# Attention two steps later in a fused attention and feed-forward kernel, its output projection behind the last down products, and the first weight scale formed in another order

## The chip, the cores and the metric

The kernel runs on one core of a Trainium2 chip. The metric is the device time of one execution in microseconds: 1605.36 us, the median of three runs (1605.04 to 1605.62). The engines' names are those of the profile: PE is the matrix engine TensorE, PEld its weight loads, DVE is VectorE, ACT is ScalarE, POOL is GpSimd, and SP is SyncE, whose queue issues every transfer (DMA) here. PSUM is the memory of eight banks into which PE writes and from which DVE and ACT fetch results ("evict" them). Moving a piece of work in one engine's program moves what stands behind it, since each engine works its program off in order.

## The reference

The input is x, 2048 rows of 576 numbers. Two blocks work on the same x, and a gate mixes them:

```python
g = sigmoid((x * gate_w).sum(-1, keepdims=True))
a = attention(x, wq, wk, wv, wo, beta)
b = (gelu(x @ w_gate) * (x @ w_up)) @ w_down      # 576 -> 4608 -> 576
return g * a + (1 - g) * b
```

The attention has 32 heads of 18 numbers. The 2048 rows form four segments of 512. Inside a segment a head has causal softmax attention. Beside that each head reads a memory M with a normalizer z, which sums phi(k) v over the segments before; the two are mixed by sigmoid(beta). The joined heads are multiplied by wo, the output projection.

## The kernel before

Numbers are held as pairs of 16-bit words, a high and a low part, and a product is three matmuls (high times high, high times low, low times high). A pair is made by an ACT copy (high) and a DVE or POOL subtraction (low); for weights this is `pair_of` (L108), after a scale that comes from the sum of the squares of the whole weight.

The work has three stages.

**Opening and projections** (about the first 220 us). PE first warms up and multiplies the unscaled x of segment 0 by the value weights (`first_words`, L509), into the banks dn, dn, V and pv for the first half of the columns (`va`) and G, U, st and st for the second half (`vb`), four blocks of 128 rows each. `put_rows` (L477) evicts such a bank: two ACT copies at once, and a DVE operation (L495, and L497 for the gate's column) that goes onto a list `later`; `finish_later` (L446) runs what is on the list. `stat_qk(j)` (L427) forms the sum of squares of one of nine weight tiles, on DVE or on ACT. `scale_sum` (L103) lets PE add those sums up over the partitions, into a bank that `spare` (L59) hands out by `turns`, and DVE reduces them and forms the scale. `make_qk(j)` (L439) makes the pair of tile j. `low_x` (L163) forms the low words of x, in three pieces. Then `project` (L450) multiplies tile j by x, into G, st, st and U in turn. The other three segments follow in the same way.

**The main loop** (from about 220 us) has 72 steps, `step(v)` (L1104). A step takes one tile f = v // 2 of 128 feed-forward columns and one half p of the rows. Four steps make a block fb of two tiles; i4 = v % 4 is the place in the block. The products with the gate and up weights use the banks V, G (named X) and U (named Y). `down` (L977) multiplies a block's hidden values (hh) by the down weights (paird), 32 calls of six matmuls each for a block, which are spread over the four steps of the next block as `early` and `late` (there are none in the first four steps). The last block's 32 follow behind the loop. The weights of the next tiles are scaled, summed and split on POOL and ACT in each step (`weights_first`, `weights_high`, `weights_low`), and `act_squares` takes squares on ACT, three of them at i4 = 1.

Between these stands attention, with k = v - LAG and LAG = 2 (L1260): in step v the scores of pair k (of its two segments) are formed (`scores`, L876, banks st and dn), DVE takes their maxima, ACT the exponentials (`powers`, L901) and the high parts, POOL the low parts (`pair_rows`, L911), SP issues two DMA transposes (`turn_rows`, L922; tiles ph to pt), and PE multiplies the result by the values (`values`, L928, bank pv) one step later for the first of the two segments and two steps later for the second. `normalize` scales the result. After four pairs the result of a group of heads is split and stored to DRAM (oa) by `result_high` (ACT, L961) and `result_low` (DVE and SP, L966). `load_head` (L842) loads the queries and keys of a pair two steps ahead, `load_v` (L859) the values of four pairs and what the memory gave (ob). Exponentials and gelu need different tables of ACT, which are loaded at each switch.

**The end.** At `LAST` = 2 * 32 + LAG + 1 attention's tiles are freed, and `turned` (L1235) fetches the stored results back, 16 blocks of 128 rows, turned by DMA (ot, ten of them at a time). `finish(0)` to `finish(4)` load the output weights (rows), take their squares, form their scale and make five pairs (wos), one call a step. Behind the loop, for each of 16 row blocks, two `down` and two output products (`chain_x`, 14 matmuls each, banks st) follow, and the block is stored.

In `tc.manual_schedule` the programs of PE, ACT, DVE and POOL have the order in which the code issues them; SP's order, and every order outside of it (the last loop, L1277 to L1288), is a scheduler's.

Of the kernel before, what the change touches and what calls it, by code (L numbers as in the profile page):

```python
# [10 lines left out]
F16 = mybir.dt.float16  # L11
# [32 lines left out]
def kernel(ctx: ExitStack, tc: tile.TileContext, xs, wqk, wv, wo, wgu, wd, beta, out):  # L44
# [58 lines left out]
    def scale_sum(i, st):  # L103
        t = wts.tile([P, 1], F32, name="sv", tag="sv", bufs=2)
        dve.tensor_reduce(t, sums(st), AX.X, OP.add)
        scale_of(i, t)

    def pair_of(t, r, sc):  # L108
        act.activation(t[:, 0, : r.shape[1]], r, AF.Copy, scale=sc)
        dve.scalar_tensor_tensor(t[:, 1, : r.shape[1]], r, sc, t[:, 0, : r.shape[1]], OP.mult, OP.subtract)  # L110

# [279 lines left out]
    with tc.tile_pool(name="prj", bufs=2, side="right", reuse_waits="tile") as pp:  # L391
# [35 lines left out]
        def stat_qk(j):  # L427
            square_sum(wst[:, 10 + j : 11 + j], raw_qk[:, j], j % 2)

# [8 lines left out]

        def make_qk(j):  # L439
            W[j] = pp.tile([P, 2, KT * P], F16, name="wp", bufs=9)  # L440
            pair_of(W[j], raw_qk[:, j], wsc[:, 0:1])

# [149 lines left out]
        with tc.manual_schedule(engines=ORDERED):  # L592
# [71 lines left out]
            for q in (2, 3):  # L664
                put_rows(0, q, 1, vb[q], usc, 1.0)
            x_raw.pop(0)
            dve.tensor_scalar(gh[:, 1], gh[:, 1], 1.0, None, OP.add)
            dve.reciprocal(gh[:, 0], gh[:, 1])
            dve.tensor_scalar(gh[:, 1], gh[:, 0], -1.0, 1.0, OP.mult, OP.add)
            finish_later()  # L670
            outscale(0, 1)

# [39 lines left out]
            def behind_rows(s, q):  # L712
                if s == 3:
                    if q < 3:
                        form_sums(1, q, -1)
                    if q == 0:
                        squares(0, 0, 0, act_square)
                    if q == 3:
                        rescale_words(2)
                        high_g(0, 0)  # L720
                        low_g(0, 0)

            def beside_products(s, j):
                if s == 0:
                    if j < 7:
                        make_qk(j + 2)
                    if j < 5:
                        make_v(j)
# [104 lines left out]
    with tc.tile_pool(name="keep", bufs=2, side="right", reuse_waits="tile") as kp, ExitStack() as tail:  # L833
# [270 lines left out]
        def step(v):  # L1104
# [137 lines left out]
        def finish(i):  # L1242
# [9 lines left out]
            if i == 2:  # L1252
                scale_sum(2, wst[:, 0:5])

                dve.tensor_scalar(gate[:, 2], gate[:, 0], wis[:, 2:3], wis[:, 3:4], OP.mult, OP.mult)
            if i >= 2:
                for k in ((0, 1), (2, 3), (4,))[i - 2]:
                    pair_of(wos[k], rows[k], wsc[:, 2:3])

        LAG = 2  # L1260
        LAST = 2 * H + LAG + 1
        with tc.manual_schedule(engines=ORDERED):
            for v in range(2 * NF):
                step(v)

                if v == LAST:
                    atn.close()
                    op_ = tail.enter_context(tc.tile_pool(name="outp", bufs=2, side="right", reuse_waits="tile"))
                if v >= LAST:
                    turned(2 * (v - LAST))  # L1270
                    turned(2 * (v - LAST) + 1)
                    finish(v - LAST)
            end_pair()
        turns.update(of=3)


        fb = NB - 1  # L1277
        for t in range(10, 16):
            turned(t)
        for t in range(16):  # L1280
            for n in range(2):
                down(fb, t, n)
            for n in range(2):
# [3 lines left out]
                dve.scalar_tensor_tensor(av, o[:, :NH], gate[:, 2, t : t + 1], av, OP.mult, OP.add)  # L1287
            sp.dma_start(out[t * P : (t + 1) * P, :], acc[:, t])  # L1288

# [39 lines left out]
```

## Time and profile before

| | us |
|---|---|
| median of three runs | 1605.36 |
| the profiled execution, its own time | 1605.14 |
| its span, first to last instruction | 1603.4 |
| PE busy in it | 1586.3 |
| ACT busy | 1166.0 |
| DVE busy | 1144.0 |
| POOL busy | 1128.2 |

A row of the timeline has the start in us from the span's start, the time in us, the engine, the line and the operation; x12 joins twelve instructions of a kind, and the brackets give the idle time of the engine just before, with what ended it. A row of the waits has the total in us, the number of times and the longest. A row of the stretches has the length, then for PE, PEld, DVE, ACT and POOL the busy time with the number of instructions, then the granted clock of TensorE, the DMA engines' busy share and GB/s. The end of a matmul is modelled: rows of back-to-back matmuls overlap, and the pace is read from one start to the next.

### The profile page before, as it was taken

The page shows a single profiled execution, that of the slowest core. Times are in us where ns is not written, and L with a number is a line of the kernel's source. Part 1 is how long each engine was busy: PE and PEld are TensorE (multiplying, and loading weights), DVE is VectorE, ACT ScalarE, POOL GpSimd, SP SyncE. Part 2 cuts the span into 40 slices and gives each one's busy share as a digit, 9 for nine tenths or more (in the row PEclk, how much of TensorE's full clock was granted, in tenths as well). Part 3 has the DMA queues.
Part 4 walks back from the last instruction along what each step waited for, and adds up shares of the span by engine and source line. Part 5 has one row for each costly group of instructions (what it writes and reads, how often), then busy time and mean ns, then how long its engine had stood idle before and what let it go on. Part 6 is the DMA issues. An engine that isn't in the chain of part 4 may idle for free.

```text
span 1603.4 us, 32611 instructions
## 1 busy us (share of the span) xinstructions
PE 1586.3 (99%) x11912; PEld 931.5 (58%) x11912; DVE 1144.0 (71%) x2957; ACT 1166.0 (73%) x1976; POOL 1128.2 (70%) x1091
## 2 busy tenths in 40 slices
PE   8999999899999999999999999999999999999999
PEld 5665754555555555555555555555555555555577
DVE  6677775677777777777777777777777777765543
ACT  6666447888888888888888888888888888863200
POOL 2233657698878888788978788888879787885200
PEclk9999999999999999999999999999999999999999
DMA  6532445688868787988877898889788887836251
GB/s 244 191 123 90 144 144 90 106 139 127 140 121 140 127 138 122 151 131 130 136 129 139 121 145 125 144 126 153 130 131 135 133 140 121 131 70 162 53 133 60
DMA packets 471872, 209.00 MB, mean 130 GB/s; under 512 B 427552, under 2 KB 436768, under 8 KB 471200
## 3 DMA queue, kind: packets, MB, share of 16 engines
q1 hardware_dynamic: 471712, 206.92, 70.8%
q8 instruction: 94, 1.54, 0.4%
q14 instruction: 66, 0.54, 0.1%
HBM read 90.99 MB, written 27.26 MB: 74 GB/s over the span
## 4 chain that ended last, share of the span: by engine, by line
PE 95%; DVE 1%; ACT 1%; DMA 1%; issue 0%; POOL 0%; SPq 0%; DVEq 0%; ACTq 0%
PE dn L985 26%; PE U L1025 17%; PE V L1025 12%; PE G L1025 11%; PE pv L940 4%; PE st L323 3%; PE st L313 3%; PE U L1032 2%; PE G L313 2%; PE dn L323 2%; PE st L888 2%; PE V L1037 1%; PE G L1037 1%; PE U L313 1%; PE G L1032 1%; PE V L1032 1%
## 5 line engine op out<-in xcount | busy, mean ns | idle before, releaser
L920 POOL TENSOR_TENSOR ph<-pf,ph 128x512 f16<-128x512 f32 (+1 forms) x256 | 353.9, 1404 | 181.5 <-ACT ph L919 179.5
L985 PE MATMUL dn<-paird,hh 128*128 128x288 f16 x3396 | 477.9, 286 | 0.5 <-POOL paird L306 0.5
L1025 PEld LDWEIGHTS <-pairg 128*128 128x128 f16 x3024 | 285.3, 98 | 308.8 <-issue 13.9
L985 PEld LDWEIGHTS <-hh 128*128 128x128 f16 x3456 | 332.8, 98 | 138.1 <-issue 2.1
L993 DVE SCALAR_TENSOR_TENSOR acc<-dn,ev,acc 128x288 f32<-128x288 f32 x534 | 274.0, 516 | 95.6 <-PE dn L985 86.9
L909 ACT ACTIVATE pf<-pf,mb,esc 128x512 f32<-128x512 f32 (+3 forms) x512 | 292.9, 642 | 6.7
L1025 PE MATMUL G<-x,pairg 128*128 128x512 f16 x864 | 209.9, 379 | 0.3 <-DVE gl L1007 0.3
L1025 PE MATMUL U<-xt,pairg 128*128 128x512 f16 x864 | 210.0, 379 | 0.0
L1012 POOL TENSOR_TENSOR hh<-gl,hh 128x512 f16<-128x512 f32 x144 | 163.8, 1158 | 56.1 <-ACT hh L1011 54.4
L896 DVE CUSTOM_DVE_ANT_0 pf<-st,mask 128x512 f32<-128x512 f32 (+2 forms) x384 | 183.9, 504 | 0.0
L294 POOL TENSOR_TENSOR pairg<-raw,pairg 128x640 f16<-128x640 f32 (+2 forms) x144 | 174.0, 1231 | 5.1 <-ACT pairg L290 5.1
L919 ACT ACTIVATE ph<-pf 128x512 f16<-128x512 f32 (+1 forms) x256 | 172.4, 720 | 0.0
L1162 DVE COPY gl<-U 128x512 f32<-128x512 f32 x72 | 49.8, 691 | 135.3 <-PE U L1025 135.3
L290 ACT ACTIVATE pairg<-raw 128x640 f16<-128x640 f32 (+2 forms) x144 | 89.5, 648 | 69.6 <-POOL raw L284 40.6
L259 POOL TENSOR_SCALAR raw<-raw,sc 128x640 f32<-128x640 f32 x72 | 135.8, 1899 | 0.0
L1015 ACT ACTIVATE gl<-gl,sc 128x512 f32<-128x512 f32 x144 | 98.5, 718 | 45.7 <-DVE gl L1181 25.5
L1025 PE MATMUL U<-x,pairg 128*128 128x512 f16 x432 | 105.4, 380 | 0.4 <-DVE gl L1181 0.4
L1025 PE MATMUL V<-xt,pairg 128*128 128x512 f16 x432 | 105.7, 381 | 0.0
L1181 DVE TENSOR_TENSOR gl<-U,gl 128x512 f32<-128x512 f32 x72 | 49.7, 690 | 78.5 <-PE U L1037 71.2
L1025 PE MATMUL V<-x,pairg 128*128 128x512 f16 x432 | 104.8, 378 | 0.4 <-ACT hh L1011 0.2
L906 ACT ACTIVATE mb<-mx,esc 128x4 f32<-128x4 f32 x128 | 37.8, 295 | 89.7 <-DVE mx L896 87.0
L1011 ACT ACTIVATE hh<-gl 128x512 f16<-128x512 f32 x144 | 82.9, 616 | 24.9 <-DVE gl L1007 24.8
(276 smaller groups left out, 2560.0 us busy)
## 6 DMA issues: line engine op xcount, KB each, us to landing
raw<-in_wgu_dram SPq DMA_DIRECT2D x36, 640.0 KB
rawd<-in_wd_dram SPq DMA_DIRECT2D x36, 288.0 KB
qk<-stage SPq DMA_DIRECT2D x36, 256.0 KB
qt<-qk SPq DMA_DIRECT2D x128, 72.0 KB
kt<-qk SPq DMA_DIRECT2D x128, 72.0 KB
vp<-vstage SPq DMA_DIRECT2D x16, 296.0 KB
vt<-vp SPq DMA_DIRECT2D x16, 296.0 KB
qt<-qk SPq DMA_DIRECT2D x128, 36.0 KB
```

The source lines that it names most:

```text
L259: pool.tensor_scalar(r, r, scl[f // 2][0][:, 0:1], None, OP.mult)
L294: pool.tensor_tensor(spot(f, *p, 1), raw_g[f][:, p[0] : p[1]], spot(f, *p, 0), OP.subtract)
L313: pe.matmul(o, w(k, a), x[:, 4 * b + k], start=n == 0, stop=False)
L896: dve.tensor_tensor_reduce(prob[a][:, COL[qi] : COL[qi + 1]], ov, mask[:, L - (qi + 1) * P :], 1.0, -3e38, OP.add, OP.max, mx[a][:, qi : q ...
L909: act.activation(r, r, AF.Exp, bias=b[:, qi : qi + 1], scale=esc[:, 0, c : c + 1])
L919: act.activation(h[:, 0, cols], p[:, cols], AF.Copy)
L920: pool.tensor_tensor(h[:, 1, cols], p[:, cols], h[:, 0, cols], OP.subtract)
L985: pe.matmul(o[:, :NH], hh[:, a, q * P : (q + 1) * P], w[:, b, n * NH : (n + 1) * NH], start=i == 0, stop=i == 5)
L993: dve.scalar_tensor_tensor(av, o[:, :NH], ev, av, OP.mult, OP.add)
L1012: pool.tensor_tensor(hh[:, 1], t, hh[:, 0], OP.subtract)
L1015: act.activation(t, o, AF.Gelu_apprx_tanh, scale=scl[f // 2][0][:, 2 + c : 3 + c])
L1025: pe.matmul(o, w[:, i, (a + k) * P : (a + k + 1) * P], x[:, b + k], start=start and k == 0 and i == 0 and b == h, stop=k == 1 and i == 1, ...
```

## The change

- The sums of squares of the q and k weights are all taken in a row, five on ACT (tiles 1, 3, 5, 6, 7) and four on DVE, and two evictions of the list are set between and behind the pieces of `low_x`. The sums of the first scale go into a dn bank (`turns.update(of=2)`) and are asked for behind the two ACT evictions of G and U. The eviction of G comes ahead of the first weight pair, the last piece of `low_x` and other evictions behind it; the pair of tile 1 is made in two parts (`pair_high`, `pair_low`, new names for the halves of `pair_of`). The three operations on `gh` move into the projections of segment 0.
- LAG is 4. The conditions of `result_high`, `result_low` and `load_v` are written in k, so that they stay at the same distance from attention. In step 4 the first piece of the down products moves behind the next product. `load_head` has no new condition: in steps 0 and 1 it is called with -2 and -1, which reads the queries and keys of the second half's pairs 30 and 31 into tiles that nobody reads.
- `finish(3)` makes the five high parts of the output weights; it is called behind the loop, and the low parts are made between the last down products. All 32 last down products come first, then all 32 output products. The last loop is inside the manual schedule. The last row block is stored in two halves.
- One `form_sums` of segment 3 each moves one row block later.

```diff
+    def pair_high(t, r, sc):
+        act.activation(t[:, 0, : r.shape[1]], r, AF.Copy, scale=sc)
+
+    def pair_low(t, r, sc):
+        dve.scalar_tensor_tensor(t[:, 1, : r.shape[1]], r, sc, t[:, 0, : r.shape[1]], OP.mult, OP.subtract)
...
-            square_sum(wst[:, 10 + j : 11 + j], raw_qk[:, j], j % 2)
+            square_sum(wst[:, 10 + j : 11 + j], raw_qk[:, j], j in (1, 3, 5, 6, 7))
...
-            stat_qk(4)
+            for j in (4, 5, 6, 8, 7):
+                stat_qk(j)
+            later.pop(0)()
             low_x(0, 1)
-            for j in (6, 5, 8, 7):
-                stat_qk(j)
-            finish_later()
-            low_x(0, 2)
+            later.pop(0)()
...
                     if qs[0] and k == 1:
-                        scale_sum(0, wst[:, 10:19])
-                        make_qk(0)
                         put_rows(0, 0, 1, vb[0], usc, 1.0)
                         put_rows(0, 1, 1, vb[1], usc, 1.0)
-                        finish_later()
-                        make_qk(1)
+                        turns.update(of=2)
+                        scale_sum(0, wst[:, 10:19])
+                        turns.update(of=3)
+                        later.pop(2)()
+                        make_qk(0)
+                        low_x(0, 2)
+                        make_qk(1, pair_high)
...
             for q in (2, 3):
                 put_rows(0, q, 1, vb[q], usc, 1.0)
+                later.pop(0)()
+                later.pop()()
+                if q == 2:
+                    make_qk(1, pair_low)
...
                 if s == 3:
-                    if q < 3:
-                        form_sums(1, q, -1)
+                    if q:
+                        form_sums(1, q - 1, -1)
...
-            done = (k - 5) // 4 if i4 == 3 and 0 <= (k - 5) // 4 < H // 2 else None
-            low = (k - 6) // 4 if i4 == 0 and 0 <= (k - 6) // 4 < H // 2 - 1 else None
+            done = (k - 5) // 4 if k % 4 == 1 and 0 <= (k - 5) // 4 < H // 2 else None
+            low = (k - 6) // 4 if k % 4 == 2 and 0 <= (k - 6) // 4 < H // 2 - 1 else None
...
-            some(fb - 1, early[:1])
+            if v != 4:
+                some(fb - 1, early[:1])
...
-            some(fb - 1, early[1:2])
+            some(fb - 1, early[0 if v == 4 else 1 : 2])
...
-            if i4 == 0:
-                load_v(fb)
+            if k >= -2 and k % 4 == 2:
+                load_v((k + 2) // 4)
...
-            if i >= 2:
-                for k in ((0, 1), (2, 3), (4,))[i - 2]:
-                    pair_of(wos[k], rows[k], wsc[:, 2:3])
-
-        LAG = 2
+            if i == 3:
+                for k in range(KT):
+                    pair_high(wos[k], rows[k], wsc[:, 2:3])
+
+
+        LAG = 4
...
-        turns.update(of=3)
-
-
-        fb = NB - 1
-        for t in range(10, 16):
-            turned(t)
-        for t in range(16):
-            for n in range(2):
-                down(fb, t, n)
-            for n in range(2):
-                o = bank("st", 2)
-                chain_x(o[:, :NH], lambda i: ot[t][:, i], lambda k, b: wos[k][:, b, n * NH : (n + 1) * NH])
-                av = acc[:, t, n * NH : (n + 1) * NH]
-                dve.scalar_tensor_tensor(av, o[:, :NH], gate[:, 2, t : t + 1], av, OP.mult, OP.add)
-            sp.dma_start(out[t * P : (t + 1) * P, :], acc[:, t])
+            turns.update(of=3)
+
+
+            fb = NB - 1
+            for t in range(turned_n, 10):
+                turned(t)
+            finish(3)
+            for t in range(16):
+                for n in range(2):
+                    down(fb, t, n)
+                if 2 <= t < 2 + KT:
+                    pair_low(wos[t - 2], rows[t - 2], wsc[:, 2:3])
+            for t in range(10, 16):
+                turned(t)
+            for t in range(16):
+                for n in range(2):
+                    o = bank("st", 2)
+                    chain_x(o[:, :NH], lambda i: ot[t][:, i], lambda k, b: wos[k][:, b, n * NH : (n + 1) * NH])
+                    av = acc[:, t, n * NH : (n + 1) * NH]
+                    dve.scalar_tensor_tensor(av, o[:, :NH], gate[:, 2, t : t + 1], av, OP.mult, OP.add)
+                    if t == 15:
+                        sp.dma_start(out[t * P :, n * NH : (n + 1) * NH], av)
+                if t < 15:
+                    sp.dma_start(out[t * P : (t + 1) * P, :], acc[:, t])
```

More of the change, by code (lines that the diff above doesn't have):

```diff
@@ L106, in scale_sum @@
         scale_of(i, t)
+    def pair_high(t, r, sc):
+        act.activation(t[:, 0, : r.shape[1]], r, AF.Copy, scale=sc)
+    def pair_low(t, r, sc):
+        dve.scalar_tensor_tensor(t[:, 1, : r.shape[1]], r, sc, t[:, 0, : r.shape[1]], OP.mult, OP.subtract)
     def pair_of(t, r, sc):
-        act.activation(t[:, 0, : r.shape[1]], r, AF.Copy, scale=sc)
-        dve.scalar_tensor_tensor(t[:, 1, : r.shape[1]], r, sc, t[:, 0, : r.shape[1]], OP.mult, OP.subtract)
+        pair_high(t, r, sc)
+        pair_low(t, r, sc)
     def outscale(c, i):
@@ L437, in make_v, with make_qk @@
             pair_of(t, raw_v[:, k], wsc[:, 1:2])
-        def make_qk(j):
-            W[j] = pp.tile([P, 2, KT * P], F16, name="wp", bufs=9)
-            pair_of(W[j], raw_qk[:, j], wsc[:, 0:1])
+        def make_qk(j, part=pair_of):
+            if j not in W:
+                W[j] = pp.tile([P, 2, KT * P], F16, name="wp", bufs=9)
+            part(W[j], raw_qk[:, j], wsc[:, 0:1])
         later = []
@@ L726, in beside_products @@
                         make_qk(j + 2)
+                    if j == 1:
+                        dve.tensor_scalar(gh[:, 1], gh[:, 1], 1.0, None, OP.add)
+                        dve.reciprocal(gh[:, 0], gh[:, 1])
+                        dve.tensor_scalar(gh[:, 1], gh[:, 0], -1.0, 1.0, OP.mult, OP.add)
+                        outscale(0, 1)
                     if j < 5:
@@ L1255, in finish @@
                 dve.tensor_scalar(gate[:, 2], gate[:, 0], wis[:, 2:3], wis[:, 3:4], OP.mult, OP.mult)
-            if i >= 2:
-                for k in ((0, 1), (2, 3), (4,))[i - 2]:
-                    pair_of(wos[k], rows[k], wsc[:, 2:3])
-        LAG = 2
+            if i == 3:
+                for k in range(KT):
+                    pair_high(wos[k], rows[k], wsc[:, 2:3])
+        LAG = 4
+        turned_n = 0
         LAST = 2 * H + LAG + 1
@@ L1269 @@
                 if v >= LAST:
-                    turned(2 * (v - LAST))
-                    turned(2 * (v - LAST) + 1)
+                    for _ in range(2):
+                        turned(turned_n)
+                        turned_n += 1
                     finish(v - LAST)
             end_pair()
-        turns.update(of=3)
-        fb = NB - 1
-        for t in range(10, 16):
-            turned(t)
-        for t in range(16):
-            for n in range(2):
-                down(fb, t, n)
-            for n in range(2):
-                o = bank("st", 2)
-                chain_x(o[:, :NH], lambda i: ot[t][:, i], lambda k, b: wos[k][:, b, n * NH : (n + 1) * NH])
-                av = acc[:, t, n * NH : (n + 1) * NH]
-                dve.scalar_tensor_tensor(av, o[:, :NH], gate[:, 2, t : t + 1], av, OP.mult, OP.add)
-            sp.dma_start(out[t * P : (t + 1) * P, :], acc[:, t])
+            turns.update(of=3)
[20 more added lines that the diff above has]
+                    sp.dma_start(out[t * P : (t + 1) * P, :], acc[:, t])
 def kernel(**inputs):
```

5 lines of the change are left out of this document (removed).

## The prediction, made before the changed kernel had run

> **What bounds the kernel now.** I read the page's busy table first, then who TensorE waits for, then stretches cut at the steps of the main loop, and last the single rows at each wait.
>
> ```profile
> PE 1586.3 (99%) x11912; PEld 931.5 (58%) x11912; DVE 1144.0 (71%) x2957; ACT 1166.0 (73%) x1976; POOL 1128.2 (70%) x1091
> ```
>
> TensorE (PE) is busy for 1586.3 of 1603.4 us. The change neither adds nor removes a matmul, so it can win only from the 17.1 us in which PE idles, and from matmuls that run slowly. Who ends that idle time (us in total, times, longest):
>
> ```profile
> PE pv L940 <- DMA pt<-ph: 5.9, 4, 2.6
> PE G L313 <- DVE gate L497: 1.3, 1, 1.3
> ...
> PE V L91 <- DVE vstage L495: 0.9, 1, 0.9
> ...
> PE st L323 <- ACT wo L109: 0.5, 1, 0.5
> PE st L323 <- DVE wo L110: 0.4, 1, 0.4
> ```
>
> The first is the probabilities that the attention's value products need; the next two belong to the opening; the last two to the output projection. The stretches below are the steps v=2, 3, 4 and 5 (length, then busy time of PE, PEld, DVE, ACT, POOL, then granted clock, DMA share, GB/s):
>
> ```profile
> 242.75:254.97 12.22, 12.01 (x58) 5.19 (x57) 5.91 (x15) 3.60 (x6) 7.85 (x9) 1.00 0.01 2
> 254.97:268.63 13.66, 12.59 (x82) 5.42 (x80) 7.76 (x24) 13.12 (x22) 9.35 (x8) 1.00 0.55 85
> 268.63:294.97 26.34, 20.65 (x148) 11.18 (x147) 13.55 (x37) 20.95 (x37) 17.09 (x13) 0.94 0.77 138
> 294.97:313.47 18.50, 18.50 (x150) 10.61 (x149) 14.74 (x43) 15.62 (x28) 15.14 (x20) 1.00 0.73 131
> ```
>
> PE idles 1.07 us in step 3 and 5.69 us in step 4, and not at all in step 5, which stands for the sixty steps behind it. In step 3 ScalarE (ACT) is the tight engine, 13.12 of 13.66 us: the steps of the first pair of feed-forward tiles have no down products, so PE needs only about 11 to 12 us for them, while attention asks ACT for as much as in a long step.
>
> **The change part by part.** All sums are against the profiled execution: 1605.14 us for a span of 1603.4, and 0.22 us under the median 1605.36.
>
> *Attention two steps later (LAG 2 to 4).* The first scores move from step 2 to step 4, so all of attention lies beside down products, in steps of about 18.5 us.
>
> ```profile
> 284.06 0.19 PE L940 MATMUL pv<-vt,pt 128*128 128x37 f16 x1 [1.65 <-DMA pt<-ph]
> 286.84 0.65 PE L940 MATMUL pv<-vt,pt 128*128 128x37 f16 x19 [2.59 <-DMA pt<-ph]
> 287.33 2.93 PE L985 MATMUL dn<-paird,hh 128*128 128x288 f16 x12
> 290.06 1.87 PE L1025 MATMUL U<-x,pairg 128*128 128x512 f16 x6
> ...
> 307.50 1.63 PE L985 MATMUL dn<-paird,hh 128*128 128x288 f16 x12
> 308.97 1.46 PE L1025 MATMUL U<-x,pairg 128*128 128x512 f16 x6
> ```
>
> The two waits are 4.24 us, and steps 3 and 4 idle 1.07 + 5.69 = 6.8 us together: minus 6.8. Behind the waits the same twelve down products take 2.93 us instead of 1.63 and the next six 1.87 instead of 1.46: 1.7 us lost to the clock of 0.94 in that stretch, which goes with the waits: minus 1.7. What is late next: step 4 now starts the chain scores, maxima, exponentials, pairs, transposes on idle engines (ACT has 18.5 - 15.6 = 2.9 us over in a full step), and its first value products come in step 5. The boundary between steps 3 and 4 still has the weight pairs of the first down products to wait for (they are moved two pieces later there for step 4 alone); bounds 0 and the 1.07 us of step 3; I take plus 0.3, as the removed exponentials are what kept ACT and GpSimd (POOL) busy there.
>
> At k = -4 and -3 the loader of heads runs with negative numbers: 16 more transfers on SyncE's (SP's) queue, for tiles nobody reads. They fall into steps 0 to 2, and step 2 shows the DMAs at 0.01 of their time: nothing. Without that cover they would hold up the first head by their issue time alone, some 2 us for each four.
>
> All that hangs on attention and not on v (values, load_v, result stores) keeps its distance to it. What shifts is the phase against the weights' work. The high part of a result, one ACT copy of 576 columns (under the 0.83 us of 640 columns below), comes in the step with three squares; 2.9 us of spare cover it. Its stores come in the step that also loads a down tile; that is the first rival below. Bounds: minus 0.3 (a lighter queue two steps later, no wait is there to win) and plus 15; I take plus 0.4, nearest to the row of the same stores today, which cause no wait.
>
> *Opening.* PE, then VectorE (DVE), then ACT:
>
> ```profile
> 20.94 2.22 PE L515 MATMUL st<-acc,raw 128*128 128x290 f32 x8
> 24.03 0.36 PE L91 MATMUL V<-wst,ones 128*128 128x9 f32 x2 [0.87 <-DVE vstage L495]
> 28.46 2.75 PE L313 MATMUL G<-x,wp 128*128 128x512 f16 x12 [1.32 <-DVE gate L497]
> ...
> 19.71 1.28 DVE L166 SCALAR_TENSOR_TENSOR x<-raw,xsc,x 128x1024 f16<-128x1024 f32 x1
> 23.38 0.51 DVE L495 SCALAR_TENSOR_TENSOR vstage<-V,usc,vstage 128x288 f16<-128x288 f32 x1
> 24.34 0.75 DVE L171 SCALAR_TENSOR_TENSOR x<-raw,xsc,x 64x512 f16<-64x512 f32 x1
> 25.13 0.17 DVE L105 TENSOR_REDUCE sv<-V 128x1 f32<-128x9 f32 x1
> 28.17 0.14 DVE L497 TENSOR_SCALAR gate<-G 128x1 f32<-128x1 f32 x1
> 26.08 0.83 ACT L109 ACTIVATE wp<-acc,wsc 128x640 f16<-128x640 f32 x1 [4.66 <-DVE wsc L100]
> ```
>
> Today the sums of the first scale go into bank V, which is free after the third eviction (23.38); the reduction stands behind L171; and the bank G of the first projection is freed only after the pair of the first weights. The new order puts the sums into a dn bank (freed by the first eviction, ahead of L166), moves one square sum of 0.8 us from DVE to ACT, sets the eviction of G ahead of the pair, and L171 and two evictions behind it. PE reaches the sums at 24.03 - 0.87 = 23.16; ACT has its three squares by about 22.3; so there is no wait, and the reduction follows at about 23.5 instead of 25.13. ACT's high part keeps its 0.95 us behind the reduction: 24.5, DVE's low part ends near 26.2. PE ends the words at 28.46 - 1.32 - 0.87 = 26.27. Both waits go: at most minus 2.2; nothing if the new order only trades the bank for the weights. I take minus 2.0, since the chain ends within 0.1 us of the moment it is needed. Later evictions (banks st, U) are needed 3 us apart each, the length of a projection tile (13 + 1 matmuls from 28.46), and DVE works some 2.2 us for one.
>
> *Output projection behind the last down products.* Today a few of its matmuls were placed into steps 69 and 70 and waited there 0.5 + 0.4 us for weights: minus 0.9. New is that the last 32 down products stand in a row, with three banks, while DVE has more to do:
>
> ```profile
> 1486.35 0.16 DVE L105 TENSOR_REDUCE sv<-dn 128x1 f32<-128x5 f32 x1
> 1487.36 0.29 DVE L1255 TENSOR_SCALAR gate<-gate,wis 128x16 f32<-128x16 f32 x1
> 1489.57 0.74 DVE L1007 SCALAR_TENSOR_TENSOR gl<-G,sc,gl 128x512 f32<-128x512 f32 x1
> L110 DVE SCALAR_TENSOR_TENSOR wo<-wor,wsc,wo 128x576 f16<-128x576 f32 x5 | 3.9, 813 | 0.5 <-ACT wo L109 0.5
> ```
>
> The scale of the output weights moves to the end of the last step: reduce to gate is 1486.35 to 1487.65, 1.3 us, then two L1007 of 0.74, then the first eviction (0.52, the last row of DVE below): 3.3 us from the reduction. PE fills three banks in 3 x 0.735 us (twelve matmuls in 1.47 us, rows above) = 2.2 and then waits about 1.1. Then five L110 stand between evictions: two evictions and one L110 are 2 x 0.52 + 0.81 = 1.85 us against PE's 1.47, five times 0.38 less what three banks hold. Together between 0 and 3.0; I take plus 1.4, as the evictions' rows overlap when they follow each other. The turned rows (DMA) have two steps and these 23.5 us to arrive; without them the projection would stand still by as much as they are late.
>
> *Last store halved.*
>
> ```profile
> 1599.78 0.52 DVE L1287 SCALAR_TENSOR_TENSOR acc<-st,gate,acc 128x288 f32<-128x288 f32 x1 [1.20 <-PE st L326]
> 1600.33 0.33 SPq L1288 DMA_DIRECT2D out_dram<-acc  x1
> ```
>
> From the issue to the end of the span are 3.1 us for 288 KB; half the bytes wait at the end: between 0 and minus 1.4; I take minus 0.3, for most of a single transfer's time doesn't hang on its size in the rows of heads of 36 and 72 KB, whose issues take alike.
>
> Sum: -6.8 - 1.7 + 0.3 + 0.4 - 2.0 - 0.9 + 1.4 - 0.3 = -9.6; 1605.14 - 9.6 = 1595.5, and against the median plus 0.2: **1595.8 us**.
>
> The row of the clock says that 4.2 us of waiting cost 1.7 us more. The Trainium skill, "TensorE: Matmul & The Clock Gate", Part 1, says that the clock halves only after an idle window of about 3.4 us. By the row in proportion the new 1.4 us at the end would cost another 0.6 and the sum be 1596.4; by the rule nothing, and it stays 1595.8.
>
> **The rivals.** *First: the transposes queue behind the stores (slower).* Rows of SP, and of PE where a time of use is meant:
>
> ```profile
> 405.42 0.38 SPq L197 DMA_DIRECT2D rawd<-in_wd_dram  x1
> 407.81 4.21 SPq L926 DMA_TRANSPOSE pt<-ph  x2
> 417.28 0.67 PE L940 MATMUL pv<-vt,pt 128*128 128x37 f16 x20
> ...
> 277.17 5.88 SPq L926 DMA_TRANSPOSE pt<-ph  x2
> ...
> 367.77 0.39 SPq L974 DMA_DIRECT2D oa<-oh  x1
> 368.21 0.57 SPq L869 DMA_DIRECT2D ob<-om  x1
> 370.96 1.99 SPq L926 DMA_TRANSPOSE pt<-ph  x1
> ```
>
> In the new queue the load of 288 KB (rawd), a store of 144 KB (oa) and a load of 144 or 288 KB (ob) stand together ahead of one pair of transposes, in every fourth step. Those transposes are issued until 412.02 and needed at 417.28, 5.3 us later. The one landing that a wait shows (286.84) came 3.8 us after its issue ended (277.17 + 5.88). So 1.5 us are free, 0.3 of them spent by SP on the added issues (0.39 + 0.57 less one head's 0.62). 288 to 432 KB at the 131 GB/s of a full step are 2.2 to 3.3 us: if the transposes wait for all of it, PE waits 1.0 to 2.1 us, some 15 times: plus 15 to 32, so 1611 or more; slower from 0.65 us each. Against it: the same oa and ob stand ahead of the transposes of 370.96 today, and no wait follows. Part of it, 0.1 to 0.4 us each, would give 1598 to 1602. The Trainium skill, "DMA: Bandwidth & Descriptors", section "Queues, rings and completion order", says that each DMA engine takes descriptors in ring order; by that rule alone it is this rival that comes.
>
> *Second: the waits only move.* The chain from scores to transposes starts two steps later and is again late: the change wins what is left, 9.6 - 8.2 = 1.4, so 1604.2. For it: the same chain was late in both of its first steps. Against it: step 5, as full of attention, has PE at 18.50 of 18.50.
>
> *Third: the opening trades one wait for another*, as DVE's program only changes order: 1597.8, inside the range.
>
> **How the numbers follow.** Forecast with its own spread (opening 0 to -2.2, end 0 to +3.0, boundary 0 to 1.1), 1593 to 1598.5: 0.80, the third rival among it. Collision in part: 0.07; in full: 0.07. Waits only move: 0.04, which lies within the 3.2 us (0.2%) that a measurement can't tell from no change. Better than 1593: 0.02. The range 1592.8 to 1600 holds the forecast and half of the partial collisions. Faster 0.80 + 0.07 + 0.02 = 0.89, same 0.04, slower 0.07.
>
> **What would show it.** Right: no pv wait of PE before step 6 and a clock of 1.00 in all slices but the end; the first projection at about 26.3 us; the two st L323 waits gone; one wait of about 1 us on dn at the fourth of the last down products; PE's idle time near 8 us. Wrong: pv waits on pt in every fourth step, waits of the projection for ot, or a step 4 or 5 with PE far under its length.

## The result and the profile after

| | before | after |
|---|---|---|
| median of ten runs each, us | 1605.20 | 1610.86 |
| lowest to highest run, us | 1604.43 to 1608.72 | 1605.34 to 1614.70 |
| the profiled execution, us | 1605.14 | 1605.34 |
| its span, us | 1603.4 | 1603.6 |

The ratio after to before is 1.0028 (95% interval 1.0016 to 1.0040): the change makes the kernel slower, by about 4.5 us by this ratio and 5.7 us by the medians, where the prediction had 9.6 us of gain. The new kernel's runs also spread over 9.4 us, those of the kernel before over 4.3 us. The profiled execution is the fastest of the ten, so its trace shows the least of what went wrong.

First the busy line of its page, and who PE waits for (us in total, times, longest):

```profile
PE 1584.4 (99%) x11912; PEld 930.1 (58%) x11912; DVE 1161.6 (72%) x2955; ACT 1165.2 (73%) x1978; POOL 1133.6 (71%) x1091
```

```profile
PE dn L902 <- DVE acc L1007: 8.0, 7, 1.2
PE st L562 <- DVE mo L553: 2.2, 1, 2.2
PE dn L999 <- DVE acc L1007: 1.2, 2, 0.8
...
PE U L1039 <- DVE gl L1196: 0.8, 1, 0.8
```

Every wait that the change set out from is gone: none for the probabilities (pv on pt), none for the first scale in the opening, none for the output weights. But DVE is 17.6 us busier with two instructions fewer, and a wait stands on top that did not exist: the last piece of the scores (L902, L888 before), which needs a dn bank, waits for a down eviction (L1007, L993 before) seven times, 8.0 us in all. Nearly all of DVE's added time lies in operations that meet one of POOL, as shown below: 11.4 us in L983, 1.2 us in L190, and 5.7 us in five short operations of the weights' scale (L225 to L231), for which PE never waits; a few others got shorter. Without the dn L902 wait PE would idle 19.2 - 8.0 = 11.2 us instead of 17.1.

The place of that wait, in the timeline of the changed kernel. A block that loses time comes first, then the next block of four steps, which doesn't:

```profile
390.73 0.52 DVE L1007 SCALAR_TENSOR_TENSOR acc<-dn,ev,acc 128x288 f32<-128x288 f32 x1 [0.74 <-PE dn L999]
391.17 2.23 DVE L983 SCALAR_TENSOR_TENSOR oh<-ob,wsc,oh 128x576 f16<-128x576 f32 x1
393.32 0.93 DVE L1007 SCALAR_TENSOR_TENSOR acc<-dn,ev,acc 128x288 f32<-128x288 f32 x2
...
389.27 2.28 POOL L300 TENSOR_TENSOR pairg<-raw,pairg 128x640 f16<-128x640 f32 x2
391.50 1.28 POOL L312 TENSOR_TENSOR paird<-rawd,paird 128x576 f16<-128x576 f32 x1
...
393.88 0.27 PE L902 MATMUL dn<-kt,qt 54*128 54x256 f16 x1 [1.14 <-DVE acc L1007]
...
466.03 0.99 DVE L983 SCALAR_TENSOR_TENSOR oh<-ob,wsc,oh 128x576 f16<-128x576 f32 x1
466.94 0.93 DVE L1007 SCALAR_TENSOR_TENSOR acc<-dn,ev,acc 128x288 f32<-128x288 f32 x2
...
464.14 2.26 POOL L300 TENSOR_TENSOR pairg<-raw,pairg 128x640 f16<-128x640 f32 x2
466.37 1.79 POOL L312 TENSOR_TENSOR paird<-rawd,paird 128x576 f16<-128x576 f32 x1
...
467.50 0.27 PE L902 MATMUL dn<-kt,qt 54*128 54x256 f16 x1
...
539.66 2.23 DVE L983 SCALAR_TENSOR_TENSOR oh<-ob,wsc,oh 128x576 f16<-128x576 f32 x1
```

L983 is `result_low`, one DVE operation in four steps. The change keeps it at its distance from attention, so among the steps of the weights it moved from i4 = 0 to i4 = 2, and there POOL makes the low parts of the gate weights' and the down weights' pairs (L300, L312) at that very time. Both outcomes have the same start: L983 begins 0.38 us before the second L300 ends. Then either L983 gets in, takes 0.99 us, and POOL's L312 takes 1.79 us instead of 1.28; or L312 gets in, and L983 takes 2.23 us and ends 0.62 us after it (391.50 + 1.28 = 392.78). In the first case too L983 ends 0.62 us behind the POOL operation that it waited for, there L300 (464.14 + 2.26 = 466.40, against 467.02). When DVE loses, the eviction behind L983 is late and PE waits 1.14 us; from L983 to L983 the four steps then take 466.03 - 391.17 = 74.86 us, against 539.66 - 466.03 = 73.63 us: 1.23 us for a lost race. There are fifteen such races in an execution (the sixteenth L983 stands alone at the end).

In the kernel before the same operation (L969) was never disturbed. The summary of its instructions (minimum, median, maximum in ns), and DVE and POOL around the first one:

```profile
L969 DVE SCALAR_TENSOR_TENSOR oh<-ob,wsc,oh x16: 808/809/810, 366.9 to 1452.2; 128x576 f16<-128x576 f32 x16
```

```profile
366.93 0.81 DVE L969 SCALAR_TENSOR_TENSOR oh<-ob,wsc,oh 128x576 f16<-128x576 f32 x1
...
363.33 2.28 POOL L294 TENSOR_TENSOR pairg<-raw,pairg 128x640 f16<-128x640 f32 x2
```

The step i4 = 0 has no down weights to split, so POOL is done at 365.61 and idle when L969 starts.

The trace of the kernel before had the sign all the same, at another operation. L166, which forms low words of x, takes 1.28 us in the three of its eight rows that no POOL operation overlaps, and 1.73 to 2.07 us in the five that meet L471 on POOL. The mean of all eight is 1679 ns:

```profile
L166 DVE SCALAR_TENSOR_TENSOR x<-raw,xsc,x 128x1024 f16<-128x1024 f32 x8 | 13.4, 1679 | 0.2
```

Another warning was in writing. The Trainium skill, "SBUF — State Buffer", section "SBUF: two separate sides", says that VectorE and GpSimd share one pair of ports into SBUF as an exclusive lock: VectorE needs it for an operation with two inputs in SBUF (against a GpSimd operation that reads SBUF) or in a mode that uses two ports, the one that starts first holds it for its whole instruction, and the other blocks fully. The rows above agree that the loser waits for the winner's end: from L983's start it is 0.38 us to the end of L300 and 1.61 us to that of L312, and L983 takes 0.18 and 1.42 us longer than its undisturbed 0.81 us, so the wait costs it all but some 0.2 us. They don't bear out that the first to start wins: by the rows L983 starts 0.33 us ahead of L312 in both outcomes. What they add is that a VectorE operation that already waits may still lose to the next of two POOL operations back to back. What decides it no run shows.

The second wait (st L562, 2.2 us) is in the last of segment 3's four row blocks. The wait of 0.8 us in the kernel before (L555, at 168.59) was in the first of them, and is gone:

```profile
179.57 1.21 DVE L357 TENSOR_TENSOR acc<-acc 128x1024 f32<-128x1024 f32 x1
180.70 2.62 DVE L190 TENSOR_SCALAR x<-x,xr 128x4608 f16<-128x4608 f16 x1
...
184.97 0.82 DVE L553 TENSOR_TENSOR mo<-st,rden 128x396 f32<-128x396 f32 x2
...
180.70 3.38 POOL L300 TENSOR_TENSOR pairg<-raw,pairg 128x640 f16<-128x640 f32 x2 [2.58 <-ACT pairg L296]
...
185.68 0.63 PE L562 MATMUL st<-ident,phi 128*128 128x128 f32 x4 [2.18 <-DVE mo L553]
```

`form_sums` (L357) was moved one row block later, where it stands ahead of the rescaling of the words (L190), which delays the recall (L542 to L553) whose bank PE needs. The rescaling takes 2.62 us, and took 1.41 in the kernel before:

```profile
182.92 1.41 DVE L184 TENSOR_SCALAR x<-x,xr 128x4608 f16<-128x4608 f16 x1
```

It now starts together with L300 on POOL and waits for it too: 1.21 us more, of the 1.40 us of the first of the two L300.

Steps 3, 4, 5 and 6 of the main loop, in the columns of the prediction's stretches:

```profile
254.59:265.41 10.82, 9.82 (x46) 4.29 (x45) 4.69 (x7) 4.24 (x7) 4.70 (x6) 1.00 0.22 68
265.41:282.87 17.46, 17.46 (x108) 9.43 (x106) 9.72 (x23) 8.88 (x17) 10.32 (x8) 1.00 0.11 34
282.87:300.86 17.99, 17.99 (x130) 10.11 (x129) 13.68 (x38) 16.35 (x30) 14.86 (x19) 1.00 0.74 115
300.86:319.21 18.35, 18.35 (x148) 10.44 (x147) 13.40 (x37) 16.00 (x29) 16.61 (x12) 1.00 0.84 107
```

Step 4 lost 5.69 us in the kernel before, at a clock of 0.94; now it and the two steps behind it lose nothing, at 1.00. Step 3 still idles 1.00 us. The opening and the end went as follows; the first row is the sums of the first scale, the second the first projection (28.46 before), the third the fourth and fifth of the 32 last down products (up to 1525 us, so eleven of their twelve matmuls):

```profile
23.13 0.29 PE L91 MATMUL dn<-wst,ones 128*128 128x9 f32 x2
...
26.09 2.76 PE L319 MATMUL G<-x,wp 128*128 128x512 f16 x12
...
1523.68 1.51 PE L999 MATMUL dn<-paird,hh 128*128 128x288 f16 x11 [0.80 <-DVE acc L1007]
```

### The profile page after: what moved, and what is told of

It is laid out like the page before. It is cut to its first block, busy times and chain, and to the rows that moved or that the text cites. A ratio compares the mean times of both kernels' runs of the same rounds, so it can differ in the third digit from the quotient of the medians.

```text
span 1603.6 us, 32623 instructions
## 1 busy us (share of the span) xinstructions
PE 1584.4 (99%) x11912; PEld 930.1 (58%) x11912; DVE 1161.6 (72%) x2955; ACT 1165.2 (73%) x1978; POOL 1133.6 (71%) x1091
## 4 chain that ended last, share of the span: by engine, by line
PE 97%; DVE 2%; issue 1%; DMA 0%; ACT 0%; SPq 0%; DVEq 0%
PE dn L999 25%; PE U L1039 17%; PE V L1039 12%; PE G L1039 11%; PE pv L954 4%; PE st L329 3%; PE st L319 3%; PE U L1046 2%; PE G L319 2%; PE dn L329 2%; PE st L902 2%; PE V L1051 1%; PE U L319 1%; PE G L1051 1%; PE V L1046 1%; PE G L1046 1%
## 5 line engine op out<-in xcount | busy, mean ns | idle before, releaser
L1007 DVE SCALAR_TENSOR_TENSOR acc<-dn,ev,acc 128x288 f32<-128x288 f32 x534 | 273.9, 516 | 88.6 <-PE dn L999 80.0
L300 POOL TENSOR_TENSOR pairg<-raw,pairg 128x640 f16<-128x640 f32 (+2 forms) x144 | 174.3, 1232 | 8.1 <-ACT pairg L296 8.1
```

The costliest lines, as they stand in the source:

```text
L300: pool.tensor_tensor(spot(f, *p, 1), raw_g[f][:, p[0] : p[1]], spot(f, *p, 0), OP.subtract)
L1007: dve.scalar_tensor_tensor(av, o[:, :NH], ev, av, OP.mult, OP.add)
```

## The experiments

Theory A was the race; B said that DVE has simply too much to do in that step, C that it is attention's distance to the weights' loads. A2 and D are about the st L562 wait, E and F about the end, G is a limit of A. Where nothing else is said, the ratio is against the kernel before on the same chip, with its 95% interval. e1 to e4 ran on one chip, e5 to e8 on a second, e9 to e12 on a third; the kernel before had medians of 1605.40, 1605.95 and 1606.08 there. So e5 and e6 are compared with e3, and e9 with e6, across chips, and the waits in the traces count for more there than the medians.

**e1: POOL's operation out of the way.**

```diff
 def weights_low(fb, i4):
...
-    if i4 >= 2:
+    if i4 == 3:
         low_d(n0 + i4 - 2)
...
+            if fb and i4 == 2:
+                low_d(2 * fb)
             if done is not None:
                 result_high(done)
```

> The changed kernel, with only the GpSimd subtraction of the down weights' pair (L312, 1.28 us) of step i4=2 moved behind the last probability pair of that step. VectorE's and TensorE's programs stay as they are. Theory A (VectorE's low part of the result, L983, reads two operands from SBUF and cannot run while a GpSimd operation runs; where L312 follows at once on L300, GpSimd may win the race and the eviction behind L983 comes 1.2 us late): all fifteen L983 take 1.0 us or less, no wait of the scores (dn L902) on the eviction is left, and the time is the profiled 1605.3 less its 8.0 us of such waits, 1597.3, with runs within 1 us of each other. Rival B (VectorE simply has one operation of 0.8 us too many in that step, whatever GpSimd does): the waits stay, and the time is 1605 to 1615 as before the edit.

Measured: 1597.66 us (1597.38 to 1600.15), 0.9952 (0.9939 to 0.9964). No dn L902 wait is left, and L983 waits for no more than the rest of L300:

```profile
L983 DVE SCALAR_TENSOR_TENSOR oh<-ob,wsc,oh x16: 807/996/1010, 391.2 to 1478.8; 128x576 f16<-128x576 f32 x16
```

DVE and PE have the same program as in the changed kernel, and with one POOL operation moved the kernel is 10 us under the changed one's 1607.48 (e11) and 13 us under its first median of 1610.86. B falls.

**e2: the operation behind the evictions.**

```diff
+            some(fb - 1, late[1:])
             if low is not None:
                 result_low(low)
-            some(fb - 1, late[1:])
```

> The changed kernel, with L983 set behind the last two down evictions of its step instead of between the first and the second of the last three. Theory A: L983 still meets L312 and some of its rows still show 1.2 to 2.2 us, but the evictions that TensorE waits for no longer stand behind it, and the two evictions of G and U that now do have 0.8 us or more to spare: 1597.3 to 1598. Rival B, too much VectorE work in the step: the wait moves on to G and U of the next step, and the time stays above 1603.

Measured: 1597.54 us (1597.13 to 1599.24), 0.9950 (0.9937 to 0.9964). The time is as expected, the way to it isn't: L983 starts only 0.12 us before L312 ends (393.39 + 1.28 = 394.67), and takes 0.81 us throughout. That fits the 0.2 us above, by which a wait costs L983 less than it lasts.

```profile
L983 DVE SCALAR_TENSOR_TENSOR oh<-ob,wsc,oh x16: 807/809/810, 394.6 to 1480.4; 128x576 f16<-128x576 f32 x16
```

```profile
394.55 0.81 DVE L983 SCALAR_TENSOR_TENSOR oh<-ob,wsc,oh 128x576 f16<-128x576 f32 x1
...
393.39 1.28 POOL L312 TENSOR_TENSOR paird<-rawd,paird 128x576 f16<-128x576 f32 x1
```

**e3: back in the old step.**

```diff
-done = (k - 5) // 4 if k % 4 == 1 and ...
-low = (k - 6) // 4 if k % 4 == 2 and ...
+done = (k - 7) // 4 if k % 4 == 3 and ...
+low = (k - 8) // 4 if k % 4 == 0 and ...
+if k == 2 * H + 1:
+    done = H // 2 - 1
...
-            if k >= -2 and k % 4 == 2:
-                load_v((k + 2) // 4)
+            if k >= 0 and k % 4 == 0:
+                load_v(k // 4)
```

> The changed kernel, with the high part of a result, its low part and the loads of the next group back in the steps i4=3, 0 and 0 where the kernel before has them (two steps later than now; the last group as now). Theory A: L983 falls beside no GpSimd operation that starts with it, takes 0.81 us as before, no dn L902 wait, 1597.3 plus or minus 0.5. A second rival C (what costs is the distance of attention to the weights' loads, not this one operation): PE still waits, and the time stays above 1602.

Measured: 1596.30 us (1596.06 to 1598.14), 0.9944 (0.9932 to 0.9957); L983 takes 0.81 us and there is no dn L902 wait. Attention starts as late as in the changed kernel and the rest of the change is in, so C falls as well.

**e4: the race alone, in the kernel before.**

```diff
-low = (k - 6) // 4 if i4 == 0 and ...
+low = (k - 8) // 4 if i4 == 2 and ...
...
-            if i4 == 0:
+            if i4 == 2:
                 load_v(fb)
```

> The kernel before, with only the low part of a result (and the loads of a group, which take its buffer) moved from step i4=0 to i4=2; attention itself starts as before. Theory A: the collision comes without the rest of the change: 7 to 15 waits of 1.14 us on the eviction, L983's counterpart between 1.0 and 2.2 us, and 1613 to 1622 us, with runs several us apart. Rival C: 1605, as attention keeps its distance to everything else.

Measured: 1620.0 us (1619.26 to 1621.15), 1.0089 (1.0075 to 1.0103), slower by 14.6 us.

```profile
L969 DVE SCALAR_TENSOR_TENSOR oh<-ob,wsc,oh x16: 809/2222/2543, 405.3 to 1466.3; 128x576 f16<-128x576 f32 x16
```

```profile
PE dn L888 <- DVE acc L993: 9.1, 8, 1.2
PE pv L940 <- DMA pt<-ph: 4.6, 5, 2.2
PE G L1025 <- DVE gl L1007: 1.6, 2, 1.4
```

Eight lost races end in the wait known from above, a ninth (2.54 us) in one on the bank G. Nine times 1.23 are 11.1 us. The profiled execution, 1619.26 us, is 13.9 us above the kernel before on this chip, so 2.8 us are not explained: two steps' distance of the loads and the clock, 0.95 instead of 0.98 between 225 and 300 us, changed with it.

**e5: the first-stage sums back in their place** (on top of e3).

```diff
-                    if q:
-                        form_sums(1, q - 1, -1)
+                    if q < 3:
+                        form_sums(1, q, -1)
```

> The kernel with the old steps of the result's parts (e3), with the first-stage sums of the second pair of chunks formed one row block earlier again, as in the kernel before. Theory A2: the wait of 2.18 us of the key transposes (st L562) comes from these sums (L357, 1.2 us) now standing ahead of the rescaling of 4608 columns (L190) and the recall on VectorE, and from L190 meeting a GpSimd operation (2.62 us instead of 1.41). With the old order the wait is 0.8 us, as in the kernel before: 1596.3 less 1.4, 1594.9. Rival D: the wait comes from the new opening, which shifts everything by 2.4 us: it stays at 2.2 us and the time at 1596.3.

Measured: 1594.73 us (1594.37 to 1595.05), 0.9931 (0.9919 to 0.9944). The wait is 0.79 us again, in the first row block as in the kernel before, and L190 takes 1.41 us: A2 holds, to 0.2 us.

**e6: the rescaling later, the five low parts apart** (on top of e3).

```diff
-                        rescale_words(2)
                         high_g(0, 0)
...
+                    if j == 5:
+                        rescale_words(2)
...
-                if 2 <= t < 2 + KT:
-                    pair_low(wos[t - 2], rows[t - 2], wsc[:, 2:3])
+                if t % 3 == 2:
+                    pair_low(wos[t // 3], rows[t // 3], wsc[:, 2:3])
```

> As e3, with the rescaling of the third chunk's words (L190) moved from the last row block to the sixth projection tile, and the five low parts of the output weights set behind every third pair of the last down products instead of five pairs in a row. Theory A2 and the account of the end (0.8 us of dn L999 waits from the five low parts): the st L562 wait and the second dn wait go: 1596.3 less 2.2 less 0.8, 1593.3. If the order on VectorE is not what sets these waits: 1596.3, or more where L190 delays the evictions of the projection.

Measured: 1594.09 us (1593.65 to 1594.55), 0.9928 (0.9915 to 0.9940). The st L562 wait is gone, its 2.2 us with it. The half about the end was wrong, as DVE and PE show:

```profile
1509.00 0.16 DVE L105 TENSOR_REDUCE sv<-dn 128x1 f32<-128x5 f32 x1
...
1510.01 0.29 DVE L1273 TENSOR_SCALAR gate<-gate,wis 128x16 f32<-128x16 f32 x1
1510.22 0.74 DVE L1022 SCALAR_TENSOR_TENSOR gl<-G,sc,gl 128x512 f32<-128x512 f32 x1
...
1511.54 0.93 DVE L1008 SCALAR_TENSOR_TENSOR acc<-dn,ev,acc 128x288 f32<-128x288 f32 x2
...
1512.10 1.63 PE L1000 MATMUL dn<-paird,hh 128*128 128x288 f16 x12 [0.80 <-DVE acc L1008]
...
1514.93 0.81 DVE L112 SCALAR_TENSOR_TENSOR wo<-wor,wsc,wo 128x576 f16<-128x576 f32 x1
```

The wait of 0.80 us stands as before, and the first low part comes only 2.8 us behind it. Ahead of the eviction that PE waits for (1511.54) stand the scale chain (1509.00 to 1510.22) and the evictions of G and U (L1022).

**e7 and e8: the opening alone, the end alone**, each in the kernel before. e7 has the diff from `pair_high` to the operations on `gh` without `form_sums`; e8 that of `finish` and of the last loops, with LAG = 2 and only `finish(0)` to `finish(2)` in the main loop.

> The kernel before with only the new order of the opening (sums of the first scale in a dn bank, one square sum on ScalarE, evictions ahead of the first pair, the gate's coefficients later). By the prediction's step: minus 2.0 (0 to minus 2.2); by the trace of the changed kernel, whose first projection starts 2.4 us earlier: 1603.0. If the opening trades one wait for another: 1605.4.

> The kernel before with only the new end: all of the output projection behind the last down products, low parts of its weights between them, last store in halves. By the prediction's steps without the late scale chain (it has two more steps here): minus 0.9 for the two st waits, plus 0.8 for the low parts between the evictions, minus 0.2 for the last store: 1605.1. If the projection then waits for its turned rows: 1608 or more.

Measured: e7 1602.97 us, 0.9982 (0.9973 to 0.9990), so 1.6 to 4.3 us faster; its first projection starts at 26.09 us. e8 1605.28 us, 0.9997 (0.9988 to 1.0006): the new end is worth nothing by itself that can be measured; its projection waits for no turned row.

**e9: the scale of the output weights behind four down products** (on top of e6).

```diff
-                    finish(v - LAST)
+                    if v < LAST + 2:
+                        finish(v - LAST)
...
-            finish(3)
             for t in range(16):
                 for n in range(2):
                     down(fb, t, n)
+                if t == 1:
+                    finish(2)
+                    finish(3)
```

> As e6, with the scale of the output weights (sum, scale chain on VectorE, gate, high parts on ScalarE) formed behind the fourth of the last down products' pairs of halves instead of at the end of the last step. In e6 the dn wait of 0.80 us was still there, although the five low parts no longer stood in a row. Theory E: it comes from the scale chain ahead of the last evictions of G and U, as the prediction had it: the wait goes, 1594.1 less 0.8, 1593.3. Rival F: it comes from those two evictions alone (0.74 us each), which stand there in any case: 1594.1.

Measured: 1593.06 us (1592.80 to 1593.32), 0.9919 (0.9905 to 0.9932); the wait of 0.80 us is gone, the two evictions are still there: E holds. With e12, which has the same time, this is the fastest kernel of the study, 13 us under the kernel before and 14 us under the changed one on the same chip (e11).

**e10: one operand in place of two.**

```diff
-dve.scalar_tensor_tensor(flat(oh[:, 1]), flat(ob), wsc[:, 3:4], flat(oh[:, 0]), OP.mult, OP.subtract)
+dve.tensor_scalar(flat(oh[:, 1]), flat(ob), wsc[:, 3:4], None, OP.mult)
```

> The changed kernel, with L983 as a scaling with one operand in SBUF in place of a scaling and subtraction with two; the low part of attention's result is thus not the difference that the reference's precision needs. Order and place are unchanged, and GpSimd's L312 still starts in the middle of it. Theory A (two operands from SBUF take the path that GpSimd also needs): all rows of L983 are alike, under 0.85 us, L312 stays at 1.28 us, no dn L902 wait, 1597.3. Rival G (any VectorE operation from SBUF to SBUF collides): rows of two lengths and 1600 to 1615.

Measured: 1605.12 us (1604.18 to 1609.48); profiled at 1609.48.

```profile
L983 DVE TENSOR_SCALAR oh<-ob,wsc x16: 509/1943/1953, 393.1 to 1491.0; 128x576 f16<-128x576 f32 x16
```

```profile
PE dn L902 <- DVE acc L1007: 10.2, 12, 0.9
```

A's expectation failed: an operation with a single input in SBUF races as well, and lost 12 of 15 in the profiled execution. It is 0.51 us long where nothing disturbs it, 0.81 with two inputs. So two inputs aren't needed for a race, and the outcome is the one that rival G foretold. Operations that read PSUM don't show it: the 534 evictions L1007 (L993 before) have a mean of 516 ns in the kernel before and after, and none of them takes over 520 ns, though 414 of those after overlap a POOL operation. The same rule of the Trainium skill names a mode of two ports beside the two inputs, which would cover this operation and L190; no run here shows in which mode they ran.

**e11: the changed kernel again.**

> The changed kernel itself once more, to relate the number of lost races to the time. Theory A with 1.23 us for each (the distance of two L983 four steps apart is 74.86 us behind a lost race, 73.63 us behind a won one): the profiled execution has 1596.7 plus 1.23 times the number of L983 rows of 2.2 us, and no run is above 1596.7 plus 15 times 1.23, 1615.2. If something else varies between runs, the two don't agree.

Measured: 1607.48 us (1605.28 to 1609.20), 1.0009 (1.0000 to 1.0018). The profiled execution, 1609.11 us, has nine lost races, so 1596.7 + 11.1 = 1607.8; 0.9 us more is a single wait for probabilities at 1225.89, and 0.4 us are left. The number of lost races differs from run to run, and with it the time.

**e12: no transfers for heads of negative number** (on top of e9).

```diff
-            load_head(k + 2)
+            if k >= -2:
+                load_head(k + 2)
```

> As e9, without the transfers for heads of negative number that the later start of attention adds (steps k=-4 and -3, for tiles that nothing reads). The prediction costed them at nothing, in steps with idle queues: the same time as e9 within 0.3 us. If they delay the loads of the first stage's end: up to 1 us faster.

Measured: 1592.86 us (1592.75 to 1593.29), e9's time: they cost nothing.

## Why the prediction was wrong, step by step

- **Attention later (-8.2): right.** Steps 4 and 5 idle nothing and the clock stays at 1.00. The boundary keeps 1.00 us of step 3 where 0.3 was taken; it was within the bounds. e5 against e7, the same opening with and without the later attention and the new end, is 1594.73 to 1602.97, minus 8.2; the new end is in it too, and e8 measured no clear gain or loss for that alone.
- **Opening (-2.0): right**, 2.4 by the first projection (28.46 to 26.09), 1.6 to 4.3 by e7.
- **Hoisted waits and the new end (-0.9 and +1.4): right in the sum, in part by luck.** 0.95 us of waits went, 0.42 + 0.80 came, the larger at the fourth down product as foretold. Its cause is the scale chain (e9), 0.80 us where about 1.1 stood; the five low parts, for which the rest of the 1.4 stood, cost nothing (e6). The 0.42 us come earlier, in the main loop (1481.43), and had no term. Neither the turned rows nor the sixteen added transfers (e12) cost anything.
- **Last store (-0.3):** from the end of the last matmul to the end of the span are 3.43 us instead of 3.63: -0.2.
- **The first rival** (transposes behind the stores) did not come: no pv wait every fourth step. Nor did the second, whose time is 1605.36 - 1.4 = 1604.0 by the prediction's own numbers, not 1604.2, nor the third (e7). None of the signs that were named for being wrong showed: the loss came from a place that no rival named.
- **The step that failed is the phase against the weights' work, +0.4 with bounds of minus 0.3 and plus 15.** It saw that what hangs on attention now falls into another step of the weights, and then costed only `result_high` on ACT and the stores on SP's queue. `result_low` on DVE is moved by the line of code beside that of `result_high`, and the prediction doesn't name it: its 0.81 us were left as they were, without regard to what POOL does at that time. What the runs showed in its place is a DVE operation that takes 2.23 us when it has to wait for POOL's L312, and an eviction behind it for which PE waits 1.14 us. It cost 7 times 1.23 = 8.6 us in the profiled run, and 14.2 us in the median one (1610.86 against 1605.34 - 8.6 = 1596.7), by estimate between 11 and 12 lost races of 15. The plus 15 in the bounds was a right size by accident: it belonged to another mechanism (the first rival), which got 7 chances in 100 in full.
- **An edit without a price:** the move of `form_sums` is in the diff and not in the sum. It cost 1.4 us (e5).

With the two terms the sum comes out: 1595.5 + 8.6 + 1.4 = 1605.5 for the profiled execution, 1605.34 measured. Without the race (e3) the kernel is at 1596.3, 0.5 us from the forecast; without the unpriced edit too (e5) it is at 1594.7, 1.1 us below it, so part of e3's closeness is two errors that cancel.

## What to carry to other kernels

When a change shifts one periodic sequence of work against another, go through every instruction of the moved sequence, on every engine, and look at what the other engines run at its new time, not only at queues and at spare time. For VectorE operations that work from SBUF to SBUF, the neighbour to look for is GpSimd: a short one in front of an eviction belongs where GpSimd is idle, or behind the evictions that the matrix engine waits for (e1, e2 and e3 are three ways, some 10 us each against e11). An operation that shows two lengths in the trace, as L166 did in the kernel before, tells of it beforehand. And a larger spread from run to run is itself a sign: here it was a race that goes either way, fifteen times a run.

## What the runs showed of the hardware that had not been expected

- Between two GpSimd operations back to back, a VectorE operation that waits for the first to end sometimes gets in (0.99 us) and sometimes loses to the second (2.23 us), from the same start to within 0.02 us: 8 won and 7 lost in the first trace, 6 and 9 in e11.
- The clock sometimes falls behind a wait of PE of 2.18 us. In e2 and e10 the stretch behind the st L562 wait had a clock of 0.62 and 0.65, and its twelve projection matmuls took 4.44 us instead of 2.75; in the changed kernel, e1, e3 and e11 the same wait left the clock at 1.00. The stretch from 186 to 190 us, first e2, then e3 (length, PE, PEld, DVE, ACT and POOL busy, clock):

```profile
186.00:190.00 4.00, 4.00 (x15) 1.83 (x15) 2.91 (x5) 0.86 (x3) 3.92 (x4) 0.62 0.42 155
```

```profile
186.00:190.00 4.00, 4.00 (x25) 2.43 (x24) 2.91 (x5) 1.23 (x4) 3.92 (x4) 1.00 0.45 167
```

The prediction weighed a rule by which only an idle window of about 3.4 us halves the clock (the Trainium skill, "TensorE: Matmul & The Clock Gate", Part 1); e2 and e10 speak against reading it as a floor for the wait. Six transposes by PE (L562 and L564) stand between the wait and those projection matmuls; even if they don't count as work for the clock, which no run here shows, the stretch in e2 is 2.9 us long (183.71 to 186.57).
